# First two pairs of a feature phase turned in 32x32 blocks through DRAM, and the plain tiles' turn moved

## The chip, the cores and the metric

The kernel runs on one core of a Trainium2 chip. The time is that of the device for one execution, in microseconds, and less is better. Beside the matrix engine TensorE (PE) the core has VectorE (DVE), ScalarE (ACT) and GpSimd (POOL); DMAs are issued by SyncE's queue (SP), some by ScalarE's. Each engine works through its own instructions in their order.

## The reference

Four layers over 2048 tokens of 576 features, alternately a Fourier mixing and an MLP, each behind a layer normalization:

```python
x = x + _A_ref(_layernorm(x), dft_seq_re, dft_seq_im, dft_hid_re, dft_hid_im)
x = x + _B_ref(_layernorm(x), w1, b1, w2, b2)
x = x + _A_ref(_layernorm(x), dft_seq_re, dft_seq_im, dft_hid_re, dft_hid_im)
x = x + _B_ref(_layernorm(x), w1, b1, w2, b2)

def _A_ref(x, sr, si, dr, di):
    a = einsum("bsd,ed->bse", x, dr)
    b = einsum("bsd,ed->bse", x, di)
    return einsum("ts,bse->bte", sr, a) - einsum("ts,bse->bte", si, b)

def _B_ref(x, w1, b1, w2, b2):
    y = _layernorm(x)
    h = gelu(einsum("bsd,df->bsf", y, w1) + b1)
    return einsum("bsf,fd->bsd", h, w2) + b2
```

The values are f32. The hidden width of the MLP is 4608.

## The kernel before

A layer here is one mixing and one MLP; there are two. In each, a **token stage** (`Sequence`) multiplies the normalized tokens by the token DFT, and then, for each half of the tokens, a **feature phase** (`hidden`) multiplies the result by the feature DFT, adds it to x and normalizes it for the MLP, and the MLP (`mlp`) follows. So there are four feature phases; in the profile the middles of the four lie near 425, 917, 1768 and 2247 us.

Every matrix operand is split in two f32r parts: a high one, which ScalarE writes (`AF.Copy`), and a low one, the rest, which VectorE subtracts (`split`, `sub`). A product is three matmuls (`PASSES`): high by high, high by low, low by high. All products of 2x2 blocks go by seven products instead of eight, so that each operand needs sums of its blocks first.

The token stage works by 2 *plain* token tiles (128 tokens each, `PLAIN`, `first_mms`), whose products are gathered in all eight PSUM banks, and 14 further tiles of seven products each: 98 *steps* of 24 matmuls, in `run`. In a step the low split of the next step but one (`low`), the high split of the one after it (`high`), the 24 matmuls (`mms`) and the handling of the result (`post`) are written down in this order. A finished tile is turned by VectorE in 32x32 blocks (`turned`, L205) and stored in DRAM (`uvd`); loaded back with its pieces exchanged it is a full transpose. The plain tiles go through `first_post` (L606, L608): four copies on ScalarE, the turn and the store. That of the first plain tile stands right behind `first_mms`, ahead of the low split of step 0 and the sums for step 1; the other one's stands in step 1. In the last tile's steps `Hidden.begin` loads the first tiles and the feature DFT for the phase that follows, and splits them.

A feature phase has eight tile steps, n = 0 to 7. In each, the turned tile n + 1 is split (`turn`, L201 on ScalarE and L198 on VectorE), tile n - 1 is normalized (`normalize`, L252) and b2 is added to it by GpSimd (L195), and TensorE runs 54 matmuls of 288 columns; then VectorE adds the result to x (L195) and takes its statistics (L223 to L226), and GpSimd makes the factors (L229 to L233). Two tile steps make a *pair*: two tiles of 128 tokens, in two halves of 288 features each, so four blocks. For the MLP a pair must be turned, so that features lie on partitions: of a block 256 features in two pieces of 128, and the last 32, the *rests*, which lie three times below each other.

In the kernel before, pairs 0 to 2 are turned by TensorE: behind tiles 2, 4 and 6 stand 8 transposes of 128x128 (L931) and 4 of the rests (L934), which GpSimd has copied together before (L917); ScalarE takes them out of PSUM (L935, L936). Then `turn_sums` writes the first parts of y (high L944, low L198) and GpSimd makes the four sums, and `turn_parts` splits those. For pair 3 VectorE makes the sums ahead of the transposes (L975, L985).

All of this is in one order by hand (`manual_schedule`): what is written first stands first in each engine's queue. All of SP's DMAs share one queue.

## Time and profile before

| | us |
|---|---|
| three runs | 2697.81 (median), 2691.66, 2698.12 |
| the profiled execution | 2693.01 |
| its span, from the first instruction to the last | 2691.1 |
| TensorE waits at the rests of a pair (L934), 8 waits in all | 15.2 |
| TensorE waits for VectorE's low splits (L198), 6 waits | 6.3 |
| all transposes of L931, 96, 0.27 each, overlapping | 12.9 |
| all transposes of L934, 48 | 8.5 |

A row of a timeline gives start, duration, engine, line, operation, the written and read tile with partitions and elements, how many instructions in a row, and in brackets the idle time of the engine before it and what ended it. A row of windows gives the stretch, then busy time and number of instructions of PE, its weight loads, DVE, ACT and POOL, then the granted clock of TensorE, the DMA engines' busy share and GB/s. A row of DMA issues gives how often, how large, and the median time from issue to landing.

### The profile page before, as it was taken

How to read it: one execution, taken by the hardware profiler on the slowest of the kernel's cores; microseconds unless marked ns; L12 is line 12 of the kernel's file. 1: busy time of each engine (PE TensorE's matmuls, PEld its weight loads, DVE VectorE, ACT ScalarE, POOL GpSimd, SP SyncE). 2: the span in 40 equal slices, each digit the busy share in tenths (PEclk: the TensorE clock that was granted, in tenths of full speed). 3: DMA queues.
4: the chain of work that ended last, by engine and by line, in shares of the span. 5: the costliest groups of instructions: out<-in, count | busy, mean ns of one | idle time of the engine just before them, and what ended most of it. 6: DMA issues, size and time to landing. Idle time of an engine off the chain costs nothing. (4 is left out here: it accounts for less than half of the span.)

```text
span 2691.1 us, 44720 instructions
## 1 busy us (share of the span) xinstructions
PE 2644.4 (98%) x17252; PEld 2479.6 (92%) x17252; DVE 1819.4 (68%) x2515; ACT 1099.5 (41%) x1773; POOL 850.6 (32%) x766
## 2 busy tenths in 40 slices
PE   9999999999999999999999999999999999999998
PEld 9999998888888988998899999988999999899998
DVE  8999976877777565556667776566555556655555
ACT  6555644544453343333344333343333324433332
POOL 5344335434443532222251000143222235322222
PEclk9999999999999999999999999999999999999999
DMA  5677675777778566666453333646666684766664
GB/s 189 238 263 244 238 259 185 258 267 274 266 278 291 162 187 195 195 217 207 156 209 121 121 121 121 204 132 194 195 191 197 193 265 133 206 193 195 192 194 152
DMA packets 223109, 544.90 MB, mean 202 GB/s; under 512 B 23584, under 2 KB 74784, under 8 KB 222752
## 3 DMA queue, kind: packets, MB, share of 16 engines
q1 hardware_dynamic: 209568, 511.94, 60.1%
q10 hardware_dynamic: 13328, 30.09, 2.9%
q8 instruction: 137, 2.24, 0.3%
q14 instruction: 76, 0.62, 0.1%
HBM read 429.87 MB, written 114.72 MB: 202 GB/s over the span
## 5 line engine op out<-in xcount | busy, mean ns | idle before, releaser
L208 PE MATMUL bank<-R 128*128 128x288 f32 (+2 forms) x16972 | 2613.2, 316 | 21.6 <-DVE R L198 6.3
L208 PEld LDWEIGHTS bank<-R 128*128 128x128 f32 x16972 | 2448.2, 189 | 182.4 <-DVE A L195 16.5
L195 DVE TENSOR_TENSOR A<-bank,A 128x576 f32<-128x576 f32 (+3 forms) x808 | 568.5, 710 | 558.2 <-PE bank L208 471.4
L198 POOL TENSOR_TENSOR R<-A,R 128x512 fp32r<-128x512 f32 (+1 forms) x286 | 373.3, 1316 | 904.6 <-ACT R L1233 877.2
L198 DVE TENSOR_TENSOR R<-A,R 128x1024 fp32r<-128x1024 f32 (+10 forms) x539 | 535.0, 1018 | 81.0 <-ACT R L944 30.7
L195 POOL TENSOR_TENSOR A<-A 128x576 f32<-128x576 f32 (+2 forms) x102 | 155.2, 1524 | 542.5 <-ACT A L687 343.9
L198 POOL TENSOR_TENSOR A<-A 128x384 f32<-128x384 f32 (+3 forms) x184 | 229.3, 1249 | 248.1 <-DVE R L198 102.2
L1172 ACT ACTIVATE bank<-bank,b1t 128x512 f32<-128x512 f32 (+1 forms) x224 | 144.9, 647 | 368.7 <-DVE bank L195 242.7
L1233 ACT ACTIVATE R<-A 128x512 fp32r<-128x512 f32 x288 | 177.0, 629 | 273.2 <-DVE A L198 123.7
L647 ACT ACTIVATE R<-A 128x1024 fp32r<-128x1024 f32 x196 | 206.1, 1053 | 120.1 <-PE bank L208 63.2
L195 DVE TENSOR_TENSOR bank<-bank,A 128x512 f32<-128x512 f32 (+1 forms) x228 | 152.2, 670 | 143.5 <-PE bank L208 142.6
L198 DVE TENSOR_TENSOR R<-bank,R 128x512 fp32r<-128x512 f32 x232 | 156.3, 676 | 4.7 <-ACT R L1233 4.2
L198 DVE TENSOR_TENSOR A<-A 128x1024 f32<-128x1024 f32 (+3 forms) x134 | 143.3, 1076 | 4.5
L1199 ACT ACTIVATE A<-bank 128x512 f32<-128x512 f32 (+1 forms) x76 | 43.7, 575 | 229.1 <-PE bank L208 229.0
L1233 ACT ACTIVATE R<-bank 128x512 fp32r<-128x512 f32 x216 | 121.2, 595 | 30.1 <-PE bank L208 30.1
L198 DVE TENSOR_TENSOR A<-bank,A 128x512 f32<-128x512 f32 x144 | 98.0, 681 | 0.0
L1172 ACT ACTIVATE A<-bank,b1t 128x512 f32<-128x512 f32 (+1 forms) x76 | 50.5, 665 | 66.5 <-DVE bank L195 66.5
L278 ACT ACTIVATE R<-A 128x256 fp32r<-128x256 f32 x126 | 52.0, 413 | 59.1 <-DMA w_parts<-R 21.8
L252 ACT ACTIVATE A<-A,moments 128x576 f32<-128x576 f32 x58 | 48.5, 860 | 52.7 <-POOL moments L233 24.6
L279 ACT ACTIVATE R<-A,power,middle 128x128 fp32r<-128x128 f32 x126 | 60.8, 483 | 0.0
L944 ACT ACTIVATE R<-A 128x768 fp32r<-128x768 f32 (+2 forms) x36 | 32.9, 946 | 56.0 <-POOL A L198 55.9
L205 DVE STREAM_TRANSPOSE A<-A 128x1152 f32<-128x1152 f32 x32 | 44.1, 1378 | 10.9 <-ACT A L606 7.6
(64 smaller groups left out, 601.6 us busy)
## 6 DMA issues: line engine op xcount, KB each, us to landing
R<-w_parts SPq DMA_DIRECT2D x504, 320.0 KB, 3.4
R<-w_parts SPq DMA_DIRECT2D x189, 576.0 KB, 3.7
A<-in_cs SPq DMA_DIRECT2D x112, 512.0 KB, 4.1
w_parts<-R SPq DMA_DIRECT2D x63, 576.0 KB, 5.3
w_parts<-R ACTq DMA_DIRECT2D x81, 320.0 KB, 3.6
uv_mid<-A SPq DMA_DIRECT2D x28, 576.0 KB, 3.0
w_parts<-R SPq DMA_DIRECT2D x45, 320.0 KB, 4.3
A<-in_w SPq DMA_DIRECT2D x72, 192.0 KB, 4.5
```

The source lines that it names most:

```text
L195: engine.tensor_tensor(dst, a, b, op=op)
L198: engine.tensor_tensor(dst, a, b, op=OP.subtract)
L205: nc.vector.transpose(block(2 * D), block(2 * D))
L208: nc.tensor.matmul(o, a, b, start=start, stop=stop, skip_group_check=True)
L252: nc.scalar.activation(dst, src, AF.Identity, bias=mv[:, 4:5], scale=mv[:, 3:4])
L278: nc.scalar.activation(t[:, 1:4:2], src[:, 0:3:2], AF.Copy)
L279: nc.scalar.activation(t[:, 2], src[:, 1], AF.Identity, bias=power[:, 2:3], scale=middle)
L647: nc.scalar.activation(self.cells[t, i](2, NP, P)[:, 0], self.source(t, i), AF.Copy)
L944: nc.scalar.activation(y[:, i, 0:3, at], x, AF.Copy)
L1172: nc.scalar.activation(dst, src, AF.Gelu_apprx_tanh, bias=bias(f))
L1199: nc.scalar.activation(up, o, AF.Copy)
L1233: nc.scalar.activation(H[q, k](2, TC)[:, 0], src, AF.Copy)
```

## The change

In a feature phase pairs 0 and 1 are no longer turned by TensorE. `normalize` writes them with the four blocks interleaved by groups of 32 features (three activations a tile instead of one), VectorE turns the 1152 columns in 32x32 blocks in place, two DMAs write the result to DRAM (`y_mid`, the rests four times), and four DMAs read it back, each 32 partitions. The write is issued at the head of tile step 2 (and 4), the reads in step 3 (and 5); `first_parts` (formerly in `turn_sums`) at the end of step 3 (5), the sums at the start of step 4 (6), `turn_parts` at its end. Both pairs use the same two buffers, `raw` and `turned_x`. Pair 2 is still turned by TensorE, with ScalarE copying its rests; pair 3 works as before on another buffer. GpSimd's addition of b2 is written down behind the first four ninths of the next tile's matmuls.

In the token stage the turn and the store of the plain tiles are taken out of `first_post` (`first_turn`) and stand in steps 1 and 3. In `Hidden.begin` the second tile's load moves two steps back, and the first turn ahead of three splits of the feature DFT.

```diff
         def post(self, t, i):
-            if i == 1:
+            if i == 2:
                 self.out = A.alloc(2 * D)
...
+        def first_turn(self, t, out):
             turned(out)
             nc.scalar.dma_start(uvd[t], out(2 * D))
+            clock[0] += 1
+            out.free()
...
                 if n == 1:
+                    self.first_turn(0, outs[0])
+                    hidden.reserve()
                     self.first_post(1, outs[1])
-                    clock[0] += 1
-                    outs[1].free()
+                if n == 3:
+                    self.first_turn(1, outs[1])
...
-            if n == 0:
-                self.load_uv(0)
-                self.load_uv(1)
+            if n in (0, 2):
+                self.load_uv(n // 2)
...
+            if n == 5:
+                drain(self.turn(0, Block(R, self.first_ut, 2 * KH * P)))
+                self.load_uv(2)
             for k in ((), (), (), (), (0, 1, 2), (3, 4, 5), (6, 7, 8))[n]:
                 self.high_d(k)
                 self.low_d(k)
-            if n == 5:
-                drain(self.turn(0, Block(R, self.first_ut, 2 * KH * P)))
-                self.load_uv(2)
...
+            if n < 4:
+                xg = tile_x.rearrange("p e (g i) -> p e g i", i=32)
+                for k in range(2):
+                    normalize(z[:, :, k:8:2], xg[:, :, 4 * k:4 * k + 4], mv)
+                normalize(z[:, :, 8], xg[:, :, 8], mv)
...
+        def write_turned(j):
+            v = raw(4 * DH)
+            turned(raw)
+            dma(yd[j][:, :, :2 * P], v[:, :8 * P].rearrange("p (c f) -> p c f", c=4))
+            dma(yd[j][:, :, 2 * P:], v[:, None, 8 * P:].to_broadcast([P, 4, P]))
+
+        def read_turned(j):
+            src = yd[j].rearrange("(q d) c f -> c d q f", q=4)
+            for c in range(4):
+                dma(turned_x(4, 3 * P)[32 * c:32 * c + 32], src[c])
...
+        def first_parts(j):
             parts(j, slice(2, 4), slice(0, 2))
             parts(j, slice(0, 1), slice(2, 3))
...
             if n:
-                drain(turn(n + 1), *ln)
-            if n >= 2 and n % 2 == 0:
-                rests(n // 2 - 1)
+                drain(turn(n + 1))
+                next(ln)
+            if n in (2, 4):
+                write_turned(n // 2 - 1)
+            if n == 6:
+                rests(2)
...
-                if n in (3, 5) and k == 2:
-                    turn_sums((n - 3) // 2)
+                if n in (3, 5):
+                    if k == 1:
+                        read_turned(n // 2 - 1)
+                    if k == 8:
+                        first_parts(n // 2 - 1)
+                if n in (4, 6):
+                    if k == 1:
+                        turn_sums(n // 2 - 2)
+                    if k == 8:
+                        turn_parts(n // 2 - 2)
+                if k == 4:
+                    next(ln, None)
...
-            if n in (3, 5):
-                turn_parts((n - 3) // 2)
-            if n >= 2 and n % 2 == 0:
-                turn_blocks(n // 2 - 1)
             if n == NP - 2:
+                turn_blocks()
+                first_parts(2)
                 turn_sums(2)
```

How this moves instructions is seen in three places. The first is VectorE in the fourth feature phase, before, from the last low splits of pair 0's first parts in tile step 3 (R is the split operands' buffer, A the working buffer, bank the PSUM):

```order
L198 TENSOR_TENSOR R<-A,R 32x128
L198 TENSOR_TENSOR R<-A,R 128x2x128
L195 TENSOR_TENSOR A<-bank,A 128x2x288
L223 BN_STATS moments<-A 128x6 x2
L224 BN_AGGR moments<-moments 128x2
L226 TENSOR_SCALAR moments<-moments 128x1
L198 TENSOR_TENSOR R<-A,R 32x4x128
L198 TENSOR_TENSOR R<-A,R 128x4x2x128
L198 TENSOR_TENSOR R<-R 128x1152
L195 TENSOR_TENSOR A<-bank,A 128x2x288
```

and the same place in the changed kernel:

```order
L199 TENSOR_TENSOR R<-A,R 32x128
L199 TENSOR_TENSOR R<-A,R 128x2x128
L196 TENSOR_TENSOR A<-bank,A 128x2x288
L224 BN_STATS moments<-A 128x6 x2
L225 BN_AGGR moments<-moments 128x2
L227 TENSOR_SCALAR moments<-moments 128x1
L199 TENSOR_TENSOR R<-R 128x1152
L206 STREAM_TRANSPOSE A<-A 128x1152
L199 TENSOR_TENSOR R<-A,R 32x4x128
L199 TENSOR_TENSOR R<-A,R 128x4x128 x2
L196 TENSOR_TENSOR A<-bank,A 128x2x288
```

The low splits that now read what came back from DRAM stand, as before, ahead of tile 3's addition from PSUM (the third row) and its statistics. Behind these the low split of tile 5 (`R<-R 128x1152`) has moved ahead of the low splits of the sums, and pair 1's turn stands between them; then comes tile 4's addition, behind it its statistics and the low split of tile 6.

The second place is SP's queue in tile steps 4 and 5 of the same phase, in the changed kernel:

```order
L193 DMA y_mid<-A 512x1x256
L193 DMA y_mid<-A 512x1x128
L193 DMA R<-uv_mid 32x4x288 x4
L193 DMA A<-x_mid 128x2x288
L193 DMA R<-w_parts 128x640 x7
L193 DMA A<-y_mid 32x4x384 x4
```

The two writes of pair 1 stand ahead of the loads for tile 7, and the reads stand behind these and behind seven weight loads of the MLP. (In the first and the third phase two weight loads stand there.)

The third is VectorE at the start of the second layer's steps, from the last split of the plain tiles' operands on, before:

```order
L198 TENSOR_TENSOR R<-A,R 128x4x288
L205 STREAM_TRANSPOSE A<-A 128x1152
L198 TENSOR_TENSOR R<-A,R 128x1024
L195 TENSOR_TENSOR A<-A 128x1024
L198 TENSOR_TENSOR A<-A 128x1024 x2
L198 TENSOR_TENSOR A<-A 128x2x288
```

and in the changed kernel:

```order
L199 TENSOR_TENSOR R<-A,R 128x4x288
L199 TENSOR_TENSOR R<-A,R 128x1024
L196 TENSOR_TENSOR A<-A 128x1024
L199 TENSOR_TENSOR A<-A 128x1024 x2
L199 TENSOR_TENSOR A<-A 128x2x288
```

The turn of the first plain tile no longer stands ahead of step 0's low split (`R<-A,R 128x1024`) and the sums behind it.

More of the change, by code (lines that the diff above doesn't have):

```diff
@@ L673, in post @@
             b = banks[4 - 4 * (t % 2) + BANK[i]][:, :DH]
-            if i == 1:
+            if i == 2:
                 self.out = A.alloc(2 * D)
-            uv, (p1, p5, p7) = self.out(2, 2, DH), (self.post_tmp(3, DH)[:, k] for k in range(3))
+            p1, p5, p7 = (self.post_tmp(3, DH)[:, k] for k in range(3))
+            uv = self.out(2, 2, DH) if i not in (1, 6) else None
             u = p1
@@ L709, in run @@
             outs.append(A.place(UV_AT + 4 * D, 2 * D) if outs[0].at < UV_AT + 4 * D else A.place(UV_AT + 6 * D, 2 * D))
-            outs[0].free()
-            hidden.reserve()
             steps = self.steps
@@ L943, in parts @@
             if high:
-                nc.scalar.activation(y[:, i, 0:3, at], x, AF.Copy)
+                for dst, src in highs:
+                    nc.scalar.activation(dst, src, AF.Copy)
             if low:
-                sub(engine, y[64:96, i, 2, at], x[64:96, :, 2], y[64:96, i, 2, at].bitcast(F32))
-                sub(nc.vector, y[:, i, 3:5, at], x[:, :, 0:2], y[:, i, 0:2, at].bitcast(F32))
-        def turn_sums(j):
-            x = t8[j](8 * DH)[:, 6 * P:].rearrange("p (b k) -> p b k", b=4)
-            b11, b12, b22, b21 = (x[:, k] for k in range(4))
+                for k, (dst, src, hi) in enumerate(lows):
+                    sub(nc.vector if k else engine, dst, src, hi.bitcast(F32))
@@ L952, in turn_sums @@
+        def first_parts(j):
             parts(j, slice(2, 4), slice(0, 2))
             parts(j, slice(0, 1), slice(2, 3))
+        def turn_sums(j):
+            if j < 2:
+                x = turned_x(12, 4, 32).rearrange("p g e t -> p e g t")
+            else:
+                x = t8(8 * DH)[:, 6 * P:].rearrange("p (b k) -> p b k", b=4)
+            b11, b12, b22, b21 = (x[:, k] for k in range(4))
             g = nc.gpsimd if j < 2 else nc.vector
@@ L987, in turn_y @@
                 yield
-            t8s.give(t8.pop(j))
-        ln = []
+        ln = iter(())
         for n in range(NP):
@@ L1044, in hidden @@
                     parts(2, slice(0, 4), slice(3, 7), high=False, engine=nc.gpsimd)
-                    t8s.give(t8.pop(2))
                 next(y_steps)
@@ L1049, in hidden @@
         add(nc.gpsimd, tile_x, tile_x, b2t(2, DH))
-        for b in h.places:
+        for b in (*h.places, t8, t9, es, b2t):
             b.free()
-        t8s.close()
-        es.free()
-        b2t.free()
         for _ in mlp:
```

78 lines of the change are left out of this document (48 added, 30 removed).

## The prediction

> **What bounds the kernel now.** I read the page's first part, then TensorE's waits, then TensorE's timeline at the places that the change touches.
>
> ```profile
> PE 2644.4 (98%) x17252; PEld 2479.6 (92%) x17252; DVE 1819.4 (68%) x2515; ACT 1099.5 (41%) x1773; POOL 850.6 (32%) x766
> PE bank L934 <- POOL A L917: 15.2, 8, 2.5
> PE bank L208 <- DVE R L198: 6.3, 6, 2.4
> ```
>
> TensorE is busy for 98% of the span, so time is won in two ways only: by taking instructions from it, or by taking away the moments in which it waits. The second and third lines are its two largest waits (total, times, longest): for VectorE's and GpSimd's preparations. The change aims at both ways. Its places in the fourth feature phase:
>
> ```profile
> 2227.66 1.03 PE L931 MATMUL bank<-ident,A 128*128 128x128 f32 x8
> 2228.53 0.60 PE L934 MATMUL bank<-ident,A 128*96 128x128 f32 x4
> 2228.88 14.63 PE L208 MATMUL bank<-R 128*128 128x288 f32 x108
> 2243.35 1.13 PE L931 MATMUL bank<-ident,A 128*128 128x128 f32 x8
> 2246.98 0.69 PE L934 MATMUL bank<-ident,A 128*96 128x128 f32 x4 [2.50 <-POOL A L917]
> 2247.37 16.17 PE L208 MATMUL bank<-R 128*128 128x288 f32 x108
> 2263.38 1.04 PE L931 MATMUL bank<-ident,A 128*128 128x128 f32 x8
> 2265.53 11.62 PE L208 MATMUL bank<-R 128*128 128x288 f32 x89
> 2277.00 1.69 PE L975 MATMUL bank<-ident,A 128*128 128x128 f32 x14
> ...
> 2236.10:2243.30 7.20, 7.20 (x56) 7.20 (x55) 3.46 (x7) 3.05 (x3) 4.78 (x7) 1.00 0.14 40
> 2247.30:2256.40 9.10, 9.10 (x59) 9.10 (x58) 4.21 (x6) 4.11 (x6) 4.63 (x7) 0.81 0.94 313
> ```
>
> Two tiles (108 matmuls) take 2243.35 - 2228.88 = 14.47 us, so one takes 7.24 and a matmul 0.134. The last two lines are windows; the third number from the end is TensorE's granted clock: 1.00 in a tile without a wait, 0.81 in the one after the wait of 2.50 us.
>
> **What goes away in a feature phase.** The turn of pair 0: 2228.88 - 2227.66 = 1.22 us. The turn of pair 1 with its wait: 2247.37 - 2243.35 = 4.02. The slow clock behind it: 2263.38 - 2247.37 - 14.47 = 1.54. Pair 2 keeps its transposes, but its rests are now copied by ScalarE: 2265.53 - 2263.38 - 1.22 = 0.93. Together 7.7 us, in four phases 31, if nothing else gets late.
>
> **What comes instead**, worked out on the fourth phase. Let Z be the start of tile 3; without the transposes that is 2227.66 of the old clock. In it the last tile's transposes began at 2277.00, Z + 49.3.
>
> ```profile
> 2225.08 0.87 ACT L252 ACTIVATE A<-A,moments 128x576 f32<-128x576 f32 x1 [1.75 <-POOL moments L233]
> L205 DVE STREAM_TRANSPOSE A<-A 128x1152 f32<-128x1152 f32 x32 | 44.1, 1378 | 10.9 <-ACT A L606 7.6
> L278 ACT ACTIVATE R<-A 128x256 fp32r<-128x256 f32 x126 | 52.0, 413 | 59.1 <-DMA w_parts<-R 21.8
> R<-uv_mid SPq DMA_DIRECT2D x4, 144.0 KB, 2.8
> uv_mid<-A SPq DMA_DIRECT2D x28, 576.0 KB, 3.0
> w_parts<-R SPq DMA_DIRECT2D x63, 576.0 KB, 5.3
> 2232.79 1.74 SPq L192 DMA_DIRECT2D R<-uv_mid  x4
> ```
>
> *The write.* The pair's second normalization starts at 2225.08, Z - 2.6. As three activations (two of 256 elements at 0.41, one of 64, by estimate 0.25) it ends at Z - 1.5; the turn of 1152 columns takes 1.38. The write is issued at Z.
>
> *The round trip.* No row shows this transfer. Two writes (512 and 256 KB in 512 pieces each) and four reads (192 KB each), the reads waiting for the writes. Four reads of 144 KB are issued within 1.74 us and land 2.8 after their issue, so the last lands 4.2 after the first. A write of 576 KB lands after 3.0 or 5.3. For a second write issued about 1 us behind the first I take 4.3 in all; the trip is 8.5. Its ends: 3.0 + 2.8 = 5.8 (every part at its quickest, the issues hidden) and 5.3 + 1 + 4.2 + 0.5 = 11. The Trainium skill ("DMA: Bandwidth & Descriptors", section on the anatomy of one DMA) gives 2.0 us fixed plus the bytes over 436 GB/s: an estimate from it is 2 x (2.0 + 1.8) = 7.6, which would take about 4 us off the total.
>
> *Who waits for it.* The order of VectorE shows that the first pair's low splits now stand ahead of the addition of tile 3, and the second piece of them ahead of the addition of tile 4; each engine works in its order. So the landing at Z + 8.5 (1.3 us into tile 4) starts a chain. Its durations:
>
> ```profile
> 2232.89 2.88 DVE L198 TENSOR_TENSOR R<-A,R 32x256 fp32r<-32x256 f32 x4
> 2244.88 0.75 DVE L195 TENSOR_TENSOR A<-bank,A 128x576 f32<-128x576 f32 x1
> 2245.66 0.82 DVE L223 BATCH_NORM_STATS2 moments<-A 128x6 f32<-128x288 f32 x2
> 2254.08 4.28 POOL L198 TENSOR_TENSOR A<-A 128x384 f32<-128x384 f32 x4 [1.89 <-DVE R L198]
> 2258.39 1.49 ACT L944 ACTIVATE R<-A 128x1536 fp32r<-128x1536 f32 x1 [6.97 <-POOL A L198]
> 2259.41 0.19 POOL L233 TENSOR_TENSOR moments<-power,moments 128x1 f32<-128x1 f32 x1
> 2259.91 1.92 DVE L198 TENSOR_TENSOR R<-A,R 32x512 fp32r<-32x512 f32 x2 [1.49 <-ACT R L944]
> 2261.75 1.35 DVE L198 TENSOR_TENSOR R<-R 128x1152 fp32r<-128x1152 f32 x1
> 2267.53 3.00 DVE L198 TENSOR_TENSOR R<-A,R 32x256 fp32r<-32x256 f32 x4 [1.91 <-ACT R L944]
> 2270.67 2.34 DVE L198 TENSOR_TENSOR A<-A 128x384 f32<-128x384 f32 x4
> ```
>
> ScalarE's two highs 1.0; VectorE's five lows 2.0 (four took 2.88 beside a busy GpSimd; alone I count less); addition and statistics 2.05; GpSimd's three small ones 1.1 (up to 2259.60); its four sums 4.28; ScalarE's highs 1.65 (1.49, now in three); the lows 1.95: 14.0, with handovers 14.4, so Z + 22.9. Behind these in VectorE's queue stand the addition and statistics of tile 4 (2.05) and then the low split of tile 6 (1.35): Z + 26.4. TensorE reaches the fifth matmul of tile 6, the first that reads it, at Z + 3 x 7.24 + 0.5 = Z + 22.2. **A new wait of 4.2 us**, longer than the one removed, with its slow clock (1.5).
>
> The second pair's reads overwrite what the first pair's last splits read, so they start at Z + 22.9 and land at Z + 27.2. From there the same seven pieces up to the highs (1.0, 2.0, 2.05, 1.1, 4.28, 1.65), the lows 1.95, addition and statistics of tile 6 2.05, pair 2's splits 3.0 and sums 2.34, addition and statistics of tile 7 2.05, and 1.6 for its deviation, normalization and first difference: 25.1, with handovers 25.5. The last tile's transposes can begin at Z + 52.7. TensorE, at Z + 49.3 - 7.7 + 5.7 = Z + 47.3, **waits 5.4**, again with 1.5 of slow clock. Loss per phase: 52.7 + 1.5 - 49.3 = 4.9.
>
> In the second and fourth phase more stands in front of the second reads: seven weight loads in SP's queue.
>
> ```profile
> 2247.38 4.57 SPq L192 DMA_DIRECT2D R<-w_parts  x7
> R<-w_parts SPq DMA_DIRECT2D x7, 320.0 KB, 5.1
> ```
>
> They are issued in 4.57 us, and 2240 KB at the window's 313 GB/s are 7.2 us of transfer. The reads come behind them: I take 4.3 us later, between 0 and 7.2. Loss in these phases 9.2. **All four: 2 x 4.9 + 2 x 9.2 = 28.2 us lost.**
>
> **The first split.** Two places, alike; the second layer's:
>
> ```profile
> 1416.14 0.53 PE L208 MATMUL bank<-R 128*128 128x288 f32 x2 [1.42 <-ACT R L647]
> 1417.75 7.48 PE L208 MATMUL bank<-R 128*128 128x288 f32 x43 [1.08 <-DVE R L198]
> 1408.86 1.38 DVE L205 STREAM_TRANSPOSE A<-A 128x1152 f32<-128x1152 f32 x1 [5.22 <-ACT A L606]
> ...
> 1417.70:1430.00 12.30, 12.25 (x81) 12.25 (x82) 10.35 (x10) 8.02 (x13) 0.66 (x1) 0.86 0.36 130
> ```
>
> VectorE idled 5.22 us in front of the turn, and the low split and the sums that TensorE waits for stood behind it. With the turn gone from there they start 6.6 us earlier, so both waits (2.5) go, and with them the clock of 0.86 over 12.3 us (1.7): 4.2, twice, 8.4 us. The turn itself, now in step 1, and the second one in step 3 stand beside steps of 24 matmuls (3.2 us), and VectorE has the 5.22 us in hand. Without that cover each would cost 1.38. The clock is where a rule speaks otherwise: the Trainium skill ("TensorE: Matmul & The Clock Gate", Part 1 on the HAM clock gate) lets the clock fall after an idle window of about 3.4 us. By it waits of 2.5 us are free of this, and the gain here would be 5.0. The windows above contradict it: 0.86 after 1.42 + 1.08, 0.81 after 2.50.
>
> **The start of the first phase.** Here the first turn moves ahead of three splits of the feature matrix.
>
> ```profile
> 382.64 17.62 PE L208 MATMUL bank<-R 128*128 128x288 f32 x119 [2.35 <-DVE R L198]
> 380.50:390.00 9.50, 7.36 (x44) 7.36 (x45) 8.01 (x11) 3.34 (x6) 1.01 (x1) 0.82 0.68 225
> 379.24 2.08 DVE L198 TENSOR_TENSOR R<-R 128x576 fp32r<-128x576 f32 x3
> ```
>
> The 2.08 us of splits now come behind what TensorE waited for: 1.9 of the 2.35 go, and 9.5 x 0.18 = 1.7 of clock, less some rest of it: 3.4 us. The first of the splits is needed 18 matmuls (2.4 us) into the tile and is done 0.7 us into it. The load for tile 1 is now issued two steps (6.4 us) later, and still five steps ahead of its use.
>
> **The sum.** 2693.0 (profiled execution) - 8.4 - 3.4 + 28.2 = 2709.4. The median of the runs shown is 4.8 above that execution and their lowest 1.3 below it, so a median would stand near 2714; I take **2712**.
>
> **Rivals.**
> *The trip is short* (faster). What decides is the landing: each us off the trip takes about 4 us off the total. At 5 us (two single landings), with weight loads that do not delay the reads and no slow clock after the last wait, the loss is 28.2 - 14 - 8.6 - 6 = about 0, and the gains of 11.8 remain: 2686. For it: transfers are quiet here, DMA share 0.14 in a tile. Against it: two landings in a row and the low splits' place ahead of the addition. It decides below a trip of some 5.5 us. Chance 0.19.
> *The waits only take the place of those removed* (same): weight loads without effect (8.6), trip 7.5 (4), the last wait without slow clock (6): 2712 - 18.6 = 2693, about 2698 from the median. Chance 0.21.
> *Worse*: the trip at 11 us (10), reads behind all of the weight loads (5.8), strided splits slower than their rows: 2728 and more. Chance 0.1.
> *The moved first split removes nothing*, since ScalarE's high part is late for another reason: 8.4 more, 2720. Chance 0.05, within the slower side.
>
> **How the numbers follow.** The forecast, with chance 0.45, spans 2706 to 2724 by itself (trip 7 to 11). About 0.3% (8 us) is what a measurement of this kernel can tell from no change: below 2690 is faster, above 2706 slower. Forecast, worse and the useless move give slower 0.60; the second rival 0.21; the first 0.19. The range goes down to the first rival's 2686 and up to 2730, which leaves about 0.1 on each side.
>
> **What would show it.** In TensorE's timeline of after: no rows of 8 and 4 transposes behind tiles 2 and 4, and waits at the first feature matmul row of 2 to 5 us in the middle of tile 6 <-VectorE, and in front of the last tile's transposes <-VectorE; windows there at a clock near 0.8. Among VectorE's waits a new one for DMA A<-y_mid of several us. If reads of y_mid land within 5 us of the write's issue, or the tiles 3 to 7 run without a wait, the chain is wrong and the kernel is faster. At the starts of the token stages the waits for L647 and L198 should be gone.

## The result, and the profile after

| | before | after |
|---|---|---|
| median of the runs | 2695.88 us (4 runs) | 2755.99 us (4 runs) |
| ratio, 95% interval | | 1.0224, 1.0206 to 1.0242 |
| span of the profiled execution | 2691.1 us | 2754.7 us |
| mean granted TensorE clock | 0.994 | 0.983 |

The change makes the kernel 60 us slower. The prediction had the sign and two of the four places at which TensorE waits, but said 2712: 16 us of a loss of 60. The page's first row and TensorE's waits, after (waits: total, times, longest):

```profile
PE 2656.1 (96%) x17156; PEld 2486.7 (90%) x17156; DVE 1820.7 (66%) x2539; ACT 1103.8 (40%) x1817; POOL 845.1 (31%) x730
PE bank L959 <- ACT A L253: 37.2, 4, 13.0
PE bank L209 <- DVE R L199: 27.8, 16, 3.4
PE bank L1020 <- issue: 12.9, 4, 3.6
```

TensorE has 96 instructions fewer (the transposes of two pairs in four phases), and the wait of 15.2 us for GpSimd's copies is gone. In its place stand four waits of up to 13.0 us in front of pair 2's transposes (L959), for the normalization L253; 27.8 us for low splits (L199), which were 6.3 before; and 12.9 in front of the last tile's transposes (L1020). TensorE's timeline of the fourth feature phase, after, shows all three:

```profile
2285.85 0.80 PE L209 MATMUL bank<-R 128*128 128x288 f32 x4 [0.17 <-ACT R L202]
2289.67 8.96 PE L209 MATMUL bank<-R 128*128 128x288 f32 x54 [3.03 <-DVE R L199]
2302.03 6.92 PE L209 MATMUL bank<-R 128*128 128x288 f32 x50 [3.39 <-DVE R L199]
2308.78 0.38 PE L959 MATMUL bank<-ident,A 128*128 128x128 f32 x2
2322.17 1.54 PE L959 MATMUL bank<-ident,A 128*128 128x128 f32 x6 [13.01 <-ACT A L253]
...
2324.22 13.22 PE L209 MATMUL bank<-R 128*128 128x288 f32 x89
2337.28 0.38 PE L1020 MATMUL bank<-ident,A 128*128 128x128 f32 x2
2340.49 2.48 PE L1020 MATMUL bank<-ident,A 128*128 128x128 f32 x12 [2.83 <-issue]
```

The number in brackets is the idle time before a row. The first two rows are tile 5 (high part, low part; the last 4 of the 54 already belong to tile 6), the third is tile 6. The same four places in every phase, read from the same view (us of waiting; the forecast's values behind them):

| phase | tile 5 | tile 6 | pair 2's transposes | last tile's transposes | sum |
|---|---|---|---|---|---|
| 1 | 3.69 | 3.41 | 5.57 | 3.54 | 16.2 |
| 2 | 3.86 | 2.64 | 11.79 | 3.58 | 21.9 |
| 3 | 3.47 | 2.38 | 6.80 | 2.98 | 15.6 |
| 4 | 3.20 | 3.39 | 13.01 | 2.83 | 22.4 |
| forecast | 0 | 4.2 | 0 | 5.4, and 4.3 more in phases 2 and 4 | 9.6, 13.9 |

The waiting sums to 76 us. Where does it come from? SP's queue in the fourth phase (start, time to issue all of the row's transfers):

```profile
2271.27 1.24 SPq L193 DMA_DIRECT2D y_mid<-A  x2
2272.57 2.77 SPq L193 DMA_DIRECT2D R<-uv_mid  x4
2275.39 0.57 SPq L193 DMA_DIRECT2D A<-x_mid  x1
2276.07 1.96 SPq L193 DMA_DIRECT2D A<-y_mid  x4
...
2293.47 1.24 SPq L193 DMA_DIRECT2D y_mid<-A  x2
2294.77 2.79 SPq L193 DMA_DIRECT2D R<-uv_mid  x4
2297.60 0.57 SPq L193 DMA_DIRECT2D A<-x_mid  x1
2298.28 3.77 SPq L193 DMA_DIRECT2D R<-w_parts  x7
2302.21 3.40 SPq L193 DMA_DIRECT2D A<-y_mid  x4
```

The first write is issued at 2271.27, which is the Z of the prediction; the second at Z + 22.2. The reads stand behind the loads of a tile, the second ones behind seven weight loads too. Landings, from the trace's record of each transfer, us after Z:

| kernel, phase | first write lands | first reads issued | last one lands | second write issued | second reads issued | last one lands |
|---|---|---|---|---|---|---|
| after, 1 | 5.6 | 6.1 | 13.7 | 23.7 | 31.4 | 39.3 |
| after, 2 | 4.5 | 4.9 | 13.3 | 23.5 | 32.5 | 44.0 |
| after, 3 | 4.5 | 5.1 | 12.1 | 22.3 | 28.3 | 38.3 |
| after, 4 | 4.5 | 4.8 | 12.0 | 22.2 | 30.9 | 42.6 |
| forecast | 4.3 | 4.3 | 8.5 | | 22.9 (27.2 in phases 2 and 4) | 27.2 (31.5) |

And VectorE, between these landings, in the fourth phase:

```profile
2284.36 1.93 DVE L199 TENSOR_TENSOR R<-A,R 32x256 fp32r<-32x256 f32 x5 [9.58 <-ACT R L985]
2286.20 0.75 DVE L196 TENSOR_TENSOR A<-bank,A 128x576 f32<-128x576 f32 x1
...
2288.26 1.36 DVE L199 TENSOR_TENSOR R<-R 128x1152 fp32r<-128x1152 f32 x1
2292.06 1.38 DVE L206 STREAM_TRANSPOSE A<-A 128x1152 f32<-128x1152 f32 x1 [2.44 <-ACT A L253]
2296.62 1.99 DVE L199 TENSOR_TENSOR R<-A,R 32x512 fp32r<-32x512 f32 x3 [3.17 <-ACT R L985]
2298.53 0.75 DVE L196 TENSOR_TENSOR A<-bank,A 128x576 f32<-128x576 f32 x1
...
2300.61 1.36 DVE L199 TENSOR_TENSOR R<-R 128x1152 fp32r<-128x1152 f32 x1
2314.98 1.93 DVE L199 TENSOR_TENSOR R<-A,R 32x256 fp32r<-32x256 f32 x5 [13.01 <-ACT R L985]
2316.82 0.75 DVE L196 TENSOR_TENSOR A<-bank,A 128x576 f32<-128x576 f32 x1
```

Read it from the bottom. The last row is tile 5's addition, from which pair 2's normalization comes. It starts as soon as the row before it is done: the second pair's first pieces, for which VectorE sat idle 13.01 us. In the same way the addition of tile 3 (second row) stands behind the first pair's pieces, and tile 5's low split (`R<-R 128x1152`, done at 2289.62) behind both; TensorE starts at 2289.67.

### The profile page after: what moved, and what is told of

It is laid out like the page before. It is cut to its first block, busy times and chain, and to the rows that moved or that the text cites. A ratio compares the mean times of both kernels' runs of the same rounds, so it can differ in the third digit from the quotient of the medians.

```text
span 2754.7 us, 44664 instructions
## 1 busy us (share of the span) xinstructions
PE 2656.1 (96%) x17156; PEld 2486.7 (90%) x17156; DVE 1820.7 (66%) x2539; ACT 1103.8 (40%) x1817; POOL 845.1 (31%) x730
## 3 DMA queue, kind: packets, MB, share of 16 engines
q1 hardware_dynamic: 222624, 524.53, 60.9%
## 4 chain that ended last, share of the span: by engine, by line
PE 59%; DVE 2%; DMA 1%; SPq 1%; issue 1%; ACT 0%; POOL 0%; DVEq 0%; POOLq 0%; ACTq 0%
PE bank L209 59%; DVE R L199 1%; SPq L193 1%; DMA R<-w_parts 0%; DVE A L196 0%; DMA R<-uv_mid 0%; DMA A<-y_mid 0%; PE bank L1020 0%; DVE A L199 0%; POOL moments L230 0%; DVE moments L224 0%; DMA A<-uv_mid 0%; ACT A L253 0%; ACT R L985 0%; PE bank L1030 0%
## 5 line engine op out<-in xcount | busy, mean ns | idle before, releaser
L209 PE MATMUL bank<-R 128*128 128x288 f32 (+2 forms) x16972 | 2625.7, 316 | 40.5 <-DVE R L199 27.8
L199 POOL TENSOR_TENSOR R<-A,R 128x512 fp32r<-128x512 f32 (+1 forms) x286 | 373.6, 1317 | 905.1 <-ACT R L1283 866.0
L199 DVE TENSOR_TENSOR R<-A,R 128x1024 fp32r<-128x1024 f32 (+7 forms) x555 | 524.7, 971 | 168.5 <-ACT R L985 123.4
L196 POOL TENSOR_TENSOR A<-A 128x576 f32<-128x576 f32 (+2 forms) x102 | 144.0, 1416 | 526.5 <-ACT A L693 340.5
L199 POOL TENSOR_TENSOR A<-A 128x384 f32<-128x384 f32 (+3 forms) x184 | 226.4, 1234 | 223.1 <-DVE R L199 95.4
L199 DVE TENSOR_TENSOR R<-bank,R 128x512 fp32r<-128x512 f32 x232 | 156.0, 675 | 4.8 <-ACT R L1283 4.2
L199 DVE TENSOR_TENSOR A<-A 128x1024 f32<-128x1024 f32 (+3 forms) x134 | 147.1, 1104 | 4.4
L253 ACT ACTIVATE A<-A,moments 128x576 f32<-128x576 f32 (+2 forms) x90 | 57.6, 689 | 131.0 <-POOL moments L234 93.5
L230 POOL TENSOR_TENSOR moments<-moments,power 128x1 f32<-128x1 f32 x32 | 43.1, 1346 | 191.1 <-DVE moments L227 191.1
L199 DVE TENSOR_TENSOR A<-bank,A 128x512 f32<-128x512 f32 x144 | 97.9, 680 | 0.0
L985 ACT ACTIVATE R<-A 128x384 fp32r<-128x384 f32 (+3 forms) x60 | 35.2, 643 | 90.8 <-DMA A<-y_mid 57.8
L206 DVE STREAM_TRANSPOSE A<-A 128x1152 f32<-128x1152 f32 x40 | 55.1, 1378 | 15.4 <-ACT A L253 12.4
```

The costliest lines, as they stand in the source:

```text
L196: engine.tensor_tensor(dst, a, b, op=op)
L199: engine.tensor_tensor(dst, a, b, op=OP.subtract)
L206: nc.vector.transpose(block(2 * D), block(2 * D))
L209: nc.tensor.matmul(o, a, b, start=start, stop=stop, skip_group_check=True)
L230: nc.gpsimd.tensor_tensor(mv[:, 3:4], mv[:, 2:3], power[:, 0:1], op=OP.pow)
L253: nc.scalar.activation(dst, src, AF.Identity, bias=mv[:, 4:5], scale=mv[:, 3:4])
```

## The experiments

Each ratio is against runs of the kernel before, taken beside those of the experiment on the same chip (medians 2693.6 to 2694.4 us).

**The parts of the change.** `stage_only` is the kernel before with the change's edits to the token stages and to `Hidden.begin` alone; some of them:

```diff
...
+        def first_turn(self, t, out):
             turned(out)
             nc.scalar.dma_start(uvd[t], out(2 * D))
...
                 if n == 1:
+                    self.first_turn(0, outs[0])
+                    hidden.reserve()
                     self.first_post(1, outs[1])
...
+                if n == 3:
+                    self.first_turn(1, outs[1])
...
-            if n == 0:
-                self.load_uv(0)
-                self.load_uv(1)
+            if n in (0, 2):
+                self.load_uv(n // 2)
...
```

> The kernel before with only the moves in the token stages (first turns split off and moved, reads of uv_mid and the first split moved); the feature phases are those of before. Theory (all of the loss of 60 us sits in the four feature phases, where start-to-start differences rise by 17, 24, 16 and 22 us): faster than before, 2680 to 2690 us, with the starts of the first phase and of layer 1's token stage some 4 us early each. Rival (the moves in the token stage of layer 0, which was 3.8 us early at its start and 1.4 late 40 us on, give everything back): 2693 to 2699.

Measured: 2685.72 us, ratio 0.9962 (0.9948 to 0.9976). That is 8.7 us less than before, as the theory said.

`feature_only` has everything else of the change (`y_mid`, the new `hidden`), and the token stages of before.

> The kernel before with only the new feature phase (two pairs turned by VectorE and through y_mid, plain tiles turned in the main loop). Theory: the whole loss and a little more, since the gains of the token stages are missing: 2760 to 2772 us. Rival (part of the loss comes from the moved turns in the token stages): below 2750.

Measured: 2764.07 us, ratio 1.0258 (1.0243 to 1.0273), in the theory's range. The parts add up: -8.7 and +69.6 make +60.9, and the whole change showed +60.1. So all of the loss is in the feature phases.

**Without the trip.** `no_reads` drops the reads and loads rows of the input into their place ahead of the first tile.

```diff
+        for c in range(3):
+            w = min(D, 12 * P - c * D)
+            dma(turned_x(12 * P)[:, c * D:c * D + w], src[c * P:(c + 1) * P, :w])
...
-                    if k == 1:
-                        read_turned(n // 2 - 1)
```

> The changed kernel without the eight reads of y_mid in a phase: the turned blocks of the first two pairs are left out, and rows of the input, loaded before the first tile, stand in their place, so nothing waits for a round trip. Every piece, sum and turn is still computed. Theory (the time goes into waiting for the round trip, in VectorE's queue): the waits in front of tiles 5 and 6 and of pair 2's transposes go, 2675 to 2690 us. Rival (the pieces cut out of 32-column blocks, and the power on GpSimd that takes 1.75 us instead of 0.55, hold the chain up by themselves): 2710 to 2740.

Measured: 2708.03 us, ratio 1.0050 (1.0035 to 1.0065). Of 60 us, 48 went: they hang on the reads. But 22 more than `stage_only` remained; the time lies between the theory's range and the rival's, 2 us below the latter. A wait at tile 6 is left with no trip at all. TensorE's timeline, fourth phase, `no_reads`:

```profile
2264.06 8.45 PE L209 MATMUL bank<-R 128*128 128x288 f32 x50 [3.62 <-DVE R L199]
```

What the 22 us are, two runs below show.

**The order of VectorE.** `parts_later` is complete, its instructions are those of the change, and the first trips are as long (12.0 to 14.0 us).

```diff
-                if n in (3, 5):
-                    if k == 1:
-                        read_turned(n // 2 - 1)
-                    if k == 8:
-                        first_parts(n // 2 - 1)
-                if n in (4, 6):
-                    if k == 1:
-                        turn_sums(n // 2 - 2)
-                    if k == 8:
-                        turn_parts(n // 2 - 2)
+                if k == 1 and n >= 4:
+                    if n % 2:
+                        turn_parts(n // 2 - 2)
+                    else:
+                        first_parts(n // 2 - 2)
+                        turn_sums(n // 2 - 2)
+                if k == 1 and n in (3, 5):
+                    read_turned(n // 2 - 1)
```

> The changed kernel with the same instructions in another order: the first pieces of a turned pair stand behind the addition and the statistics of their tile and the low split of the next, and the later pieces half a tile to a tile later. Theory (VectorE, in order, holds the addition of tile 3 behind pieces that wait for the first trip, so the second trip starts only after the first): the second write is issued 14 us behind the first instead of 22 to 24, the waits in a phase fall from 20 us to about 5, total near 2700 (2693 to 2712). Rival (the trips themselves, 12 to 20 us from issue to last landing, are too long wherever the pieces stand): waits only move, 2735 or more.

Measured: 2706.17 us, ratio 1.0040 (1.0025 to 1.0055), in the theory's range. The second write is issued at Z + 14.3 to 15.6, as said, and ScalarE's wait for the reads all but vanishes. The wait of ScalarE's highs for `y_mid`, in the changed kernel and then in this one:

```profile
ACT R L985 <- DMA A<-y_mid: 57.8, 8, 10.3
```

```profile
ACT R L985 <- DMA A<-y_mid: 1.7, 4, 0.8
```

50 us come back by order alone, with first trips as long. The second reads land at Z + 35.1 to 36.2 and hardly anything waits for them any more. What a trip costs is decided by what stands behind the instruction that waits for it. A wait of 5.1 us at pair 2's transposes stays in every phase; the runs without a trip below explain it.

**What stands ahead of the reads.** `weights_behind` moves only the weight loads, `reads_first` moves the reads ahead of all loads of their tile.

```diff
-            if n == NP - 3:
-                next(mlp)
...
                     if k == 1:
                         read_turned(n // 2 - 1)
+                        if n == NP - 3:
+                            next(mlp)
```

> The changed kernel with the first weight loads of the following matrix stage (7 in phases 2 and 4, 2 in phases 1 and 3) issued behind the second reads of y_mid instead of ahead of them. Theory (the difference between the phases, 22 to 24 us lost in phases 2 and 4 against 16 to 17 in 1 and 3, is those loads): the waits at pair 2's transposes in phases 2 and 4 fall from 11.8 and 13.0 to 5 to 7, in phases 1 and 3 by 1 to 2; 2736 to 2746 us. Rival (the weights come late instead, waits <-DMA w_parts at the start of the matrix stage): 2750 to 2758.

Measured: 2734.22 us, ratio 1.0150 (1.0133 to 1.0166): 22 us less than the changed kernel, more than the theory said. The second reads of phases 2 and 4 land at Z + 35.5 and 34.3 instead of 44.0 and 42.6, and pair 2's transposes wait there for 2.89 and 2.06 us instead of 11.79 and 13.01, less than the 5 to 7 expected. TensorE's timeline of the fourth phase, `weights_behind`:

```profile
2275.65 8.96 PE L209 MATMUL bank<-R 128*128 128x288 f32 x54 [3.03 <-DVE R L199]
2288.01 9.53 PE L209 MATMUL bank<-R 128*128 128x288 f32 x50 [3.40 <-DVE R L199]
...
2299.81 0.88 PE L959 MATMUL bank<-ident,A 128*128 128x128 f32 x6 [2.06 <-ACT A L253]
```

The waits at tiles 5 and 6 stay as long in this phase, as they must, since they do not hang on the second trip.

```diff
+            if n in (3, 5):
+                read_turned(n // 2 - 1)
             h.load(n + 2)
...
-                    if k == 1:
-                        read_turned(n // 2 - 1)
```

> The changed kernel with the four reads of y_mid of each pair issued at the head of their tile, ahead of the loads of uv_mid, x and the weights in SyncE's queue; nothing else moves. Theory (reads stand behind 5 to 13 other loads in that queue, so a trip takes 12 to 20 us): first trips fall from 12.0 to 13.7 us to about 8.5, second reads land 28 to 30 us after the first write instead of 38 to 44, the wait at tile 5 goes, a wait of 3 to 4 stays at tile 6, pair 2's transposes wait 1 to 4 instead of 5.6 to 13.0: 2705 to 2722 us. Rival (the loads that now stand behind SyncE's wait for the write come too late for the splits): waits <-DMA uv_mid appear and the time stays above 2735.

Measured: 2718.69 us, ratio 1.0091 (1.0076 to 1.0106), inside the theory's range. The first reads land at Z + 9.9 to 11.1, the second ones at 30.8 to 32.2, each some 2 us later than expected. TensorE's timeline, fourth phase, `reads_first`:

```profile
2260.23 6.91 PE L209 MATMUL bank<-R 128*128 128x288 f32 x50 [0.76 <-DVE R L199]
...
2272.98 8.52 PE L209 MATMUL bank<-R 128*128 128x288 f32 x50 [3.97 <-DVE R L199]
...
2283.75 0.88 PE L959 MATMUL bank<-ident,A 128*128 128x128 f32 x6 [2.04 <-ACT A L253]
```

With first trips near the length that the prediction assumed (8.5), the wait at tile 5 is small and the one at tile 6 is 3.97 us, near the prediction's 4.2. That is in part luck: the trip took 10.1 us here, TensorE came to tile 6 some 2.7 us late by smaller waits, and `no_reads` waits 3.62 us there without a trip. The rival was not idle: ScalarE waits 34.2 us in all for `uv_mid` here (19.6 in the changed kernel).

**What is left without a trip.** `no_reads_later` is `no_reads` in the order of `parts_later`.

> The changed kernel without the reads of y_mid (rows of the input stand in their place, the turned blocks of two pairs are left out) and with the order of the run in which the pieces stand behind the additions. It has no trip and no pieces in front of an addition that it could wait for. Theory (what the run without reads still loses, 22 us against the run with the token stages alone, is the later pieces standing in front of an addition and waiting for GpSimd's sums): 2662 to 2682 us, faster than the token stages alone. Rival (the smaller cuts of the pieces, 32 columns at a time, and three instructions for one cost it by themselves): 2695 to 2710.

Measured: 2700.39 us, ratio 1.0024 (1.0015 to 1.0034). That is 6 us less than `parts_later`: with the pieces in this order the reads cost no more than that. The theory missed and the rival's range held, but the trace speaks against the rival's reason. TensorE's wait in the fourth phase of `no_reads_later`, and then GpSimd, ScalarE and VectorE ahead of it, a timeline each:

```profile
2268.76 1.54 PE L962 MATMUL bank<-ident,A 128*128 128x128 f32 x6 [4.92 <-ACT A L253]
```

```profile
2251.23 5.28 POOL L199 TENSOR_TENSOR A<-A 128x384 f32<-128x384 f32 x4 [4.97 <-DVE R L199]
2256.47 1.43 POOL L196 TENSOR_TENSOR A<-A 128x576 f32<-128x576 f32 x1
2257.85 0.55 POOL L230 TENSOR_TENSOR moments<-moments,power 128x1 f32<-128x1 f32 x1
```

```profile
2258.97 0.87 ACT L253 ACTIVATE A<-A,moments 128x576 f32<-128x576 f32 x1 [8.76 <-POOL moments L234]
2259.75 1.65 ACT L988 ACTIVATE R<-A 128x512 fp32r<-128x512 f32 x3
```

```profile
2261.50 1.99 DVE L199 TENSOR_TENSOR R<-A,R 32x512 fp32r<-32x512 f32 x3 [6.95 <-ACT R L988]
2263.41 0.75 DVE L196 TENSOR_TENSOR A<-bank,A 128x576 f32<-128x576 f32 x1
```

GpSimd's sums stand ahead of tile 4's power, so its normalization is late; ScalarE's highs stand behind that; and the lows stand ahead of tile 5's addition. The expectation had overlooked both. `no_reads_last` moves them; its edit against `no_reads_later`:

```diff
-                if k == 1 and n >= 4:
-                    if n % 2:
-                        turn_parts(n // 2 - 2)
-                    else:
+                if k == 1:
+                    if n in (4, 6):
                         first_parts(n // 2 - 2)
-                        turn_sums(n // 2 - 2)
+                    if n == 6:
+                        turn_sums(1)
+                    if n == 7:
+                        turn_parts(1)
...
             next(ln)
+            if n == 4:
+                turn_sums(0)
+            if n == 5:
+                turn_parts(0)
```

> As the earlier run without reads of y_mid (rows of the input in place of the turned blocks of two pairs, which are left out), with the first pair's sums behind the power of their tile and its later pieces behind the addition of the next. Theory (the earlier run without reads kept GpSimd's sums ahead of a power, and pieces ahead of the addition of tile 5: pair 2's transposes waited 4.9 there): these waits go, 2668 to 2686 us. Rival (the pieces cost as instructions): 2695 to 2705, as before.

Measured: 2682.54 us, ratio 0.9957 (0.9942 to 0.9972), in the theory's range: the order was the cause. Pair 2's transposes wait 0.3 us in the whole kernel. But it is no faster than `stage_only` (the intervals overlap). At tile 6 it is 4 to 6 us ahead of `stage_only`, and gives this back where the MLP starts: TensorE waits 11.7 us in four phases for ScalarE's highs of the last pieces, and some 2 us a phase right behind that for their lows.

```profile
PE bank L209 <- ACT R L988: 11.7, 4, 3.3
```

**The whole change in a better order.** `two_places` is complete: pieces behind the additions, sums behind the power, reads ahead of the loads, and a place of its own for each pair's turned blocks, so that the second reads wait only for their write. `two_places_loads` puts the first reads behind the loads again.

```diff
-        raw, turned_x = Block(A, t8.at, 4 * DH), Block(A, t9.at, 12 * P)
+        raw = Block(A, t8.at, 4 * DH)
+        turned_xs = Block(A, t9.at + 6 * P, 12 * P), Block(A, t8.at + 4 * DH, 12 * P)
...
+            if n == 3:
+                read_turned(0)
             h.load(n + 2)
...
-                if n in (3, 5):
+                if n == 4:
                     if k == 1:
-                        read_turned(n // 2 - 1)
+                        first_parts(0)
                     if k == 8:
-                        first_parts(n // 2 - 1)
-                if n in (4, 6):
-                    if k == 1:
-                        turn_sums(n // 2 - 2)
-                    if k == 8:
-                        turn_parts(n // 2 - 2)
+                        read_turned(1)
+                if n == 6 and k == 8:
+                    turn_parts(1)
...
             next(ln)
+            if n == 4:
+                turn_sums(0)
+            if n == 5:
+                turn_parts(0)
+                first_parts(1)
+                turn_sums(1)
```

> The changed kernel, complete, with every piece of a turned pair behind the additions and statistics it stood ahead of, GpSimd's sums behind the power of the tile, the reads ahead of the loads, and a place of its own for each pair's turned blocks, so that the second reads wait only for their write. Theory (the loss is queueing: three places where something that waits for a trip or for GpSimd's sums stands ahead of the addition of a tile, and the second trip behind the first pair's last piece): the waits of the feature phases fall to those of a few tenths, 2665 to 2684 us, below the token stages alone (2686). Rival (the turned pair's chain of highs, lows, sums, highs, lows, 25 us without any trip, doesn't fit beside three tiles of 7.1 us in any order): 2690 to 2705.

Measured: 2705.70 us, ratio 1.0038 (1.0023 to 1.0052): a miss, and within 1 us of the rival's range. ScalarE's waits name another reason than the rival did:

```profile
ACT R L202 <- DMA R<-uv_mid: 26.3, 6, 7.8
ACT R L202 <- DMA A<-uv_mid: 23.7, 7, 7.5
```

SP waits for the write ahead of the loads, so the operands of a tile two steps on come late.

> As the complete run with a place for each pair, but the first pair's reads of y_mid stand behind the loads of their tile again, as in the changed kernel. Theory (with the reads ahead, the loads of uv_mid came late: ScalarE waited 50 us in all for them, up to 7.8 at a time, and the second normalization and write hung on that): waits for uv_mid shrink, the first trip is 12 to 14 us again but nothing of VectorE stands behind it before the next tile; 2688 to 2700 us, about even with before. Rival (what is left is the chain to the last tile, too late in any order): 2700 to 2708.

Measured: 2693.39 us, ratio 0.9998 (0.9988 to 1.0008), in the theory's range. The waits for `uv_mid` fall to 28.1 us in all and no wait for reads of `y_mid` is left. The same work as the changed kernel's takes 63 us less and is even with the kernel before; it is still 8 more than `stage_only`.

**The slow power.** In the changed kernel GpSimd's power of a tile takes 1.61 to 1.75 us in 21 of 32 cases. `pow_alone` makes VectorE wait for it:

```diff
-        nc.gpsimd.tensor_tensor(mv[:, 4:5], mv[:, 0:1], mv[:, 3:4], op=OP.mult)
-        nc.gpsimd.tensor_tensor(mv[:, 4:5], power[:, 2:3], mv[:, 4:5], op=OP.subtract)
+        nc.vector.tensor_tensor(mv[:, 4:5], mv[:, 0:1], mv[:, 3:4], op=OP.mult)
+        nc.vector.tensor_tensor(mv[:, 4:5], power[:, 2:3], mv[:, 4:5], op=OP.subtract)
```

> The changed kernel with the two small operations behind the power (mean times scale, and its negative) on VectorE instead of GpSimd, so that VectorE waits for the power and its subtraction of two SBUF operands can't run beside it. Theory (the power takes 1.75 us where such a subtraction starts within 0.1 us of it, and 0.55 elsewhere): all powers of the feature phases take 0.55 to 0.6, normalizations come about 1.2 earlier and low splits 0.9 later; total 2748 to 2758 us, hardly another. Rival (the power is slow for another reason): its times stay at 1.6 to 1.75.

Measured (one run): 2750.07 us. All 32 powers take 0.55 to 0.56 us, so the collision is real. What it costs is not settled: this one run is 6 us below the changed kernel's median, whose own runs span 5 us, and the edit also makes VectorE wait.

## Why the prediction was wrong in size

**Right in two places of three: the token stages and the start of the first phase.** Forecast 8.4 + 3.4 = 11.8 us; `stage_only` gained 8.7, with an interval of 6.5 to 14.0. Starts of same-numbered matmuls tell where: 3.0 us at the first phase (forecast 3.4), 4.6 at the second layer's start (forecast 4.2). At the first layer's start up to 4.6 us were won too, but 0.5 was left of that 45 us on, so the other 4.2 of the forecast did not last. Two windows of the kernel before suggest why:

```profile
100.00:370.00 270.00, 270.00 (x2044) 270.00 (x2043) 250.65 (x253) 153.09 (x274) 103.64 (x66) 1.00 0.74 251
1425.00:1700.00 275.00, 275.00 (x2082) 275.00 (x2082) 197.41 (x188) 109.47 (x139) 22.25 (x25) 1.00 0.37 124
```

VectorE (third number) is busy for 250.65 of 270 us in the first layer's token stage and for 197.41 of 275 in the second's: in the first there is hardly room for what was moved in. That is read from the trace, not tried.

**Right: the mechanism in the feature phases.** VectorE's queue holds the addition of a tile behind pieces that wait for DRAM. `parts_later` showed it by reordering alone (-50 us). The chain behind the second landing was right too. Its end, the last tile's transposes, in the fourth phase of `weights_behind` and then of `reads_first`:

```profile
2318.14 2.79 PE L1020 MATMUL bank<-ident,A 128*128 128x128 f32 x12 [3.57 <-issue]
```

```profile
2302.08 2.79 PE L1020 MATMUL bank<-ident,A 128*128 128x128 f32 x12 [3.55 <-issue]
```

The second landings of these phases are at 2291.58 and 2275.48, so the transposes came 26.56 and 26.60 us behind them; in the changed kernel it is 26.6 too (2313.9 to 2340.49). The same in all phases:

| | second landing, us after Z, phases 1 to 4 | sum | from there to the last transposes |
|---|---|---|---|
| forecast | 27.2, 31.5, 27.2, 31.5 | 117.4 | 25.5 |
| after | 39.3, 44.0, 38.3, 42.6 | 164.3 | 26.5 to 26.6 |
| `weights_behind` | 36.6, 35.5, 35.5, 34.3 | 141.9 | 26.5 to 26.6 |
| `reads_first` | 31.4, 32.2, 30.8, 31.8 | 126.2 | 26.6 |

Against the changed kernel the landings of `weights_behind` and `reads_first` are 22.4 and 38.1 us earlier in sum, and their profiled executions 23.0 and 38.2 us shorter (2733.54 and 2718.37 against 2756.53). In these three kernels the time follows the second landing.

**Wrong: the second trip.** The step that failed is "they start at Z + 22.9 and land at Z + 27.2", with "4.3 us later" for the weight loads. The reads were issued at Z + 28 to 32.5 and landed at Z + 38 to 44, 11 to 12.5 us later than the 27.2 and 31.5 of the forecast, 46.9 in four phases. The time came out 44 above the forecast. In the fourth phase:
- The first pair's last pieces were done, and the place free, 4.4 us late (Z + 27.3 instead of 22.9): 3.5 from the first trip, 12.0 instead of 8.5, and 1.15 from GpSimd's three small operations (2.25 instead of 1.1, the slow power). The 3.5 also made the wait at tile 5 that the forecast did not have. Even at the head of the queue, in `reads_first`, the first trip took 9.9 to 11.1; the prediction's shorter estimate of 7.6 was further off.
- But the reads did not wait for the place. SP's rows above have no gap from the second write to the reads: the write, the tile's loads and the seven weight loads took 8.7 us to issue, and the reads followed at Z + 30.9, 3.6 us after the place was free. In the other phases SP's queue has no gap there either. So the second write, at Z + 22.2, and the queue behind it set the start, and the forecast has no time for that write. It is late because pair 1's turn waits for tile 3's normalization, and tile 3's addition stands behind the pieces of the first trip.
- The reads took 3.40 us to issue instead of 1.7, and each landed 8.0 to 8.9 us after its issue instead of 2.8. The forecast took its durations from transfers in a quiet queue; these stood behind seven weight loads and the tile's own. From the last pieces to the landing it took 15.3 us (27.3 to 42.6), where the forecast gave the reads 4.3 and the weight loads 4.3.

`weights_behind` measures the weight loads ahead of the reads: in all phases together they cost 22 us, where the forecast had 8.6, and nothing for the two loads in phases 1 and 3.

**Missed, but not what made the loss: where TensorE meets the chain first.** The forecast followed the second pair to the last tile's transposes (wait 5.4; measured 2.8 to 3.6). Pair 2's transposes come earlier and hang on the same landing by way of tile 5's addition, statistics and normalization: from landing to transpose 8.3 us (2313.9 to 2322.2). By the forecast's own landing at Z + 31.5 that would have been Z + 39.8, with TensorE there at Z + 34.6: 5 us, at a place the text did not look at. With the landing as it was, it is the largest wait of the kernel, 37.2 us in all. Yet the last transposes still waited in every phase, and they came 26.5 to 26.6 us after the landing whatever TensorE had waited before. So the waits ahead of them, and the slow clock behind those, only shorten this last wait. The forecast's way of counting with the measured landing and chain (42.6 + 26.6 + 1.5 - 49.3) gives a loss of 21.4 us for this phase instead of 9.2; by the starts of its matmuls it lost 22.4.

**The slow clock.** Two times 1.5 us a phase were priced. Windows behind the four waits of the fourth phase (the third number from the end is the clock):

```profile
2289.70:2298.00 8.30, 8.30 (x51) 8.30 (x52) 2.75 (x4) 4.16 (x7) 6.10 (x8) 0.79 0.39 119
2302.00:2309.10 7.10, 7.08 (x52) 6.90 (x52) 0.00 (x0) 0.87 (x1) 2.19 (x4) 1.00 1.00 327
2322.20:2332.00 9.80, 9.80 (x56) 9.76 (x57) 4.59 (x10) 4.80 (x8) 5.11 (x6) 0.72 0.12 27
2340.50:2345.00 4.50, 4.50 (x24) 4.16 (x25) 4.23 (x8) 2.46 (x6) 3.03 (x4) 0.62 0.02 4
```

8.3 x 0.21 + 9.8 x 0.28 + 4.5 x 0.38 = 6.2 us, twice what was priced; the last term, the only one behind the last transposes, is 1.7, near the 1.5 of the forecast. TensorE's own account of the phase agrees: 22.4 of waits and 6.2 of clock, less the 7.7 that the prediction took away, make 20.9.

**The rivals.** *The trip is short* and *the waits only take the place of those removed* are out: the first trip took 12.0 to 13.7 us. *Worse* had the right signs (trip at 11, reads behind all weight loads) with 2728 us and a chance of 0.1; with the trip still longer and the landing of each read up to 9 us after its issue, even that end was too low. *The moved first split removes nothing* is out for the second layer (4.6 us won) and nearly came true for the first (0.5 left).

**Could the idea pay?** Its gross gain is real, about 5 us at tile 6. Yet `no_reads_last`, with no trip at all, is no faster than `stage_only`: in this order the pieces of the turned pairs end too late for the MLP. The fastest complete version here leaves the feature phases alone: `stage_only`, 2685.7 us.

## What to carry to other kernels

Price a wait by what stands behind the waiting instruction in its engine's queue, and a transfer by what stands ahead of it in its own: the same instructions with first trips as long took 2756 or 2706 us by order alone, and 2693 with a second place for the turned blocks. Give each transfer of a chain the time of its own issue; here the second write had none. Waits that hang on one landing do not add up: the last of them decides, and the ones ahead of it are taken out of it. And time a part of a change alone: here a gain of 9 us was hidden under a loss of 70.

## What the runs showed of the hardware

A GpSimd power on 128 x 1 elements took 0.55 us alone and 1.71 to 1.75 when VectorE had started a subtraction of two operands in SBUF (1.36 us) 0.03 to 0.06 us earlier; with that ordered away, 32 of 32 took 0.55 or 0.56. The power of tile 3 in the fourth phase, beside the subtraction at 2288.26 shown above:

```profile
2288.32 1.71 POOL L230 TENSOR_TENSOR moments<-moments,power 128x1 f32<-128x1 f32 x1 [9.62 <-DVE moments L227]
```

The Trainium skill ("SBUF — State Buffer", section on who interferes with whom) says that such a VectorE instruction and a GpSimd instruction that reads SBUF block each other; the trace agrees for GpSimd's side.

A wait does not always bring the slow clock. Behind the wait of 3.39 us at tile 6 in the fourth phase 50 matmuls took 6.92 us at clock 1.00 (rows above); behind the wait of 3.41 at the same place in the first phase, 9.39:

```profile
434.62 9.39 PE L209 MATMUL bank<-R 128*128 128x288 f32 x50 [3.41 <-DVE R L199]
```

In `weights_behind` it is the other way round: 6.92 us in the first phase and 9.53 in the fourth, both behind a wait of 3.40. So the place does not decide it, and no run here tells what does.
